# A windowed attention with a channel mix behind it: one small load is added on ScalarE's queue, and the emission of the plan moves out of the block that fixed its order

## The chip, the cores and the metric

The kernel runs on one core of a Trainium2 chip. The metric is device time in microseconds (us) of one execution. Before the change three runs took 165.81, 166.41 and 166.73 us; their median is 166.41 us.

The core has five engines, each with its own stream of instructions: TensorE (PE in the profile, its weight loads PEld), VectorE (DVE), ScalarE (ACT), GpSimd (POOL) and SyncE (SP), which here does nothing but issue DMA transfers. A transfer is issued by the instruction stream of an engine (SPq, ACTq) and carried out by 16 DMA engines that all queues share.

## The reference, cut to what matters

There are 4 batches, 8 heads, 768 positions and a head size of 64. A position sees the first 4 positions (the sinks) and the 128 up to itself (the window). The output of the attention, heads side by side as 512 features, goes into a channel mix with a step back in time.

```python
keep = is_sink | in_window                      # rel >= 0 and rel < 128, or position < 4
a = softmax(where(keep, q @ k.T / 8, -1e9))
x = (a @ v)                                     # heads side by side: [4, 768, 512]
xk = mu_k * x + (1 - mu_k) * x_prev             # x_prev: x one position earlier
xr = mu_r * x + (1 - mu_r) * x_prev
out = sigmoid(xr @ w_r) * (maximum(xk @ w_k, 0) ** 2 @ w_v)
```

## The kernel before, in words

**Tiles.** The work is cut into 12 units u, a batch and a block of 256 positions each. For a unit, `load` (lines 289 to 341) fetches 256 positions of q, k and v for all heads. `prepare` casts them to bf16 and turns q and k so that the head size lies on the partitions: by TensorE with an evacuation (lines 576 and 589), or, for k from u = 4 and q from u = 8 on, by a DMA transpose that SyncE issues (line 562). `attend` makes the scores (line 721), their exponential on ScalarE (line 775), the mask on VectorE (line 789; units 0 and 1 have it as a bias added by TensorE, line 728), the product with v (line 808) and the division (lines 822 and 825). `mix` turns the result (line 849, or by DMA transpose at line 869 for u = 9 to 11) and blends it with its neighbour in time (lines 877 and 888). `ffn` makes the three products: keys (line 939, with relu at 949 or 953 and the square at 963 or 967), gate (line 979, tanh at 985) and values (line 997; line 909 for the very last half), the last step on VectorE (line 1006, 919) and the store (lines 1013 and 924).

**Weights** come as float32 (line 354) and are cast (lines 501 to 507). Their three staging tiles `w32` serve later as result tiles too: line 244 adds their 12 slices to the pool `ob`. That is why the profile calls most result tiles w.

**The plan.** Nothing is issued while these functions run. Each calls `P.op`, which appends an operation to a list: its engine, a closure that emits its instructions, and what it takes and holds. `Plan.run` (line 173) then does two things. It gives every buffer its slot from the written-out list `SLOTS`, so each tile and each PSUM bank has a fixed sequence of users. And it walks the list `ORDER`, a written-out order of all operations on all engines, and emits each one; a negative entry emits a filling matmul on a tile of zeros (`warm`, line 1018). In ORDER the stores of line 1013 stand far behind the operations that make their tiles: all stores but one stand behind the last loads.

**What turns emission into the order on the chip.** Tile, the framework below, finds from the tiles that each instruction reads and writes what has to wait for what, and sets the semaphores. The order of the instructions on one engine can come from two places. In a block `with tc.manual_schedule():` each engine issues its instructions in the order in which they were emitted. Outside such a block Tile's own scheduler chooses: it plays the program through in its own model of the machine, and when an engine is free there, it gets the instruction emitted earliest among those that are ready. On the chip every engine then works through its stream in order, and waits at an instruction whose inputs are not there. Before the change, `P.run()` stands in that block (line 1039), and with it all but the tiles' allocation.

**The start.** On ScalarE's queue the first instructions are two loads of mu (line 374), 4 rows of 128 numbers each, into rows 0 to 7 and columns 384 to 511 of `early`, which is result tile 2 (line 369). The bias of units 0 and 1 lies in other columns of the same tile (lines 371 and 372). Behind the two loads comes the exponential on two numbers (line 384), which loads the activation table. SyncE starts with the loads of k and q of unit 0 (line 337).

Of the kernel before, what the change touches and what calls it, by code (L numbers as in the profile page):

```python
# [185 lines left out]
def kernel(  # L186
# [14 lines left out]
    nc = tc.nc  # L201
    B, H, S, D = q.shape
# [13 lines left out]
    P = Plan()  # L216
# [152 lines left out]
    early = P.pools["ob"][2]  # L369
# [3 lines left out]
    for i, src in enumerate((moe_mu_k, moe_mu_r)):  # L373
        P.op("ACT", 500.0, lambda i=i, src=src: nc.scalar.dma_start(
            out=rows8[NC * i:NC * i + NC, :], in_=src.rearrange("(c p) -> c p", p=128)), -100,
# [660 lines left out]
    ffn(U - 1, 10 * U + FFN_AFTER)  # L1036
    with tc.manual_schedule():
        nc.vector.memset(warm, 0.0)  # L1038
        P.run()


# [33 lines left out]
```

## Time and profile before

| | |
|---|---|
| median of 3 runs | 166.41 us (165.81 to 166.73) |
| the profiled execution | 166.11 us |
| its span, first to last instruction | 164.3 us |
| TensorE clock granted, mean | 0.999 |
| DMA | 79,042 packets, 34.60 MB |

The profile is that of one execution. A group of instructions is named by its line, engine and operation, with the tile it writes, an arrow, and the tiles it reads; x48 is how many there are. A row by stage gives the stretch, its length, and for each engine its busy time and in brackets how many instructions began there, then the granted TensorE clock, the mean busy share of the 16 DMA engines and the GB/s that they moved. A row of waits reads: who waited, for whom, us in total, how often, the longest. A row of the timeline reads: start, duration, engine, line and operation. In the rows of one line or one tile the three numbers between slashes are the shortest, median and longest duration in ns, and after them the first and last start in us.

### The profile page before, as it was taken

What the parts mean: (1) busy time and instruction counts of PE and PEld (TensorE: products, weight loads), DVE (VectorE), ACT (ScalarE), POOL (GpSimd) and SP (SyncE); (2) the same over time, 40 slices, a digit from 0 to 9 for tenths busy, and PEclk for the clock granted to TensorE, in tenths of its full rate; (3) what the DMA queues carried; (4) which work ended last, traced back from release to release, by engine and by line L of the source; (5) the groups of instructions that cost most, each with busy time, mean ns of one, the idle gap of its engine ahead of it and who ended that gap; (6) DMA issues with size and microseconds to landing.
All of it is one profiled execution on the core that took longest, in us unless ns stands there. A gap on an engine that the chain in (4) does not pass through costs nothing.

```text
span 164.3 us, 4195 instructions
## 1 busy us (share of the span) xinstructions
PE 158.4 (96%) x1603; PEld 102.6 (62%) x1603; DVE 145.4 (89%) x381; ACT 131.2 (80%) x218; POOL 13.5 (8%) x38
## 2 busy tenths in 40 slices
PE   6999889999999999999999999999999999999992
PEld 2455568866467587577566775856575765664851
DVE  5259999999999999989999999999999999789752
ACT  3277999999999999999999999997668759163240
POOL 6409300010000000060000000000000000000000
PEclk9999999999999999999999999999999999999999
DMA  4999999999969896999999887986996955077743
GB/s 120 247 305 311 348 335 355 301 354 210 228 154 270 135 240 148 234 198 167 224 216 157 188 156 163 235 146 150 199 123 136 362 149 200 0 90 297 262 185 128
DMA packets 79042, 34.60 MB, mean 211 GB/s; under 512 B 67112, under 2 KB 73520, under 8 KB 79024
## 3 DMA queue, kind: packets, MB, share of 16 engines
q1 hardware_dynamic: 79008, 34.35, 86.3%
q8 instruction: 12, 0.20, 0.6%
q14 instruction: 6, 0.05, 0.1%
q10 hardware_dynamic: 16, 0.00, 0.0%
HBM read 24.12 MB, written 6.29 MB: 185 GB/s over the span
## 4 chain that ended last, share of the span: by engine, by line
PE 79%; ACT 8%; SPq 4%; DMA 3%; issue 2%; DVE 1%; POOL 1%; DVEq 0%; ACTq 0%; POOLq 0%
PE bank L997 23%; PE bank L939 23%; PE bank L979 12%; PE bank L808 6%; PE sc L721 6%; SPq L337 3%; DMA qs<-in_q_dram 3%; PE bank L576 2%; ACT e L775 2%; PE bank L849 2%; ACT rl L949 1%; PE bank L763 1%; ACT qt L589 1%; PE bank L909 1%; PE bank L1018 1%
## 5 line engine op out<-in xcount | busy, mean ns | idle before, releaser
L775 ACT ACTIVATE e<-sc 128x1024 bf16<-128x1024 f32 (+1 forms) x48 | 46.1, 994 | 1.8 <-PE sc L721 1.7
L939 PE MATMUL bank<-xk,wk_sb 128*128 128x256 bf16 x384 | 47.1, 273 | 0.0
L997 PE MATMUL bank<-wv_h,kk 128*128 128x512 bf16 x184 | 43.1, 379 | 0.1
L939 PEld LDWEIGHTS <-wk_sb 128*128 128x128 bf16 x384 | 36.4, 98 | 7.4 <-issue 0.4
L949 ACT ACTIVATE rl<-bank 128x512 bf16<-128x512 f32 x40 | 24.2, 625 | 8.6 <-PE bank L939 7.1
L997 PEld LDWEIGHTS <-kk 128*128 128x128 bf16 x184 | 17.1, 98 | 17.8 <-issue 0.4
L789 DVE TENSOR_TENSOR e<-e,mask 128x1024 bf16<-128x1024 bf16 (+1 forms) x40 | 25.4, 642 | 0.7 <-ACT e L775 0.5
L979 PE MATMUL bank<-wr_sb,xr 128*128 128x512 bf16 x96 | 23.7, 379 | 0.0
L888 DVE SCALAR_TENSOR_TENSOR xk<-td,mu_all,xt 128x256 bf16<-128x256 bf16 x48 | 22.4, 483 | 0.3
L888 DVE SCALAR_TENSOR_TENSOR xr<-td,mu_all,xt 128x256 bf16<-128x256 bf16 x48 | 22.1, 475 | 0.2
L967 ACT ACTIVATE kk<-rl 128x512 bf16<-128x512 bf16 x29 | 18.3, 664 | 4.2 <-DVE rl L953 4.0
L985 ACT ACTIVATE th<-bank 128x512 f32<-128x512 f32 x24 | 15.1, 646 | 5.7 <-PE bank L979 5.7
L825 DVE TENSOR_TENSOR x<-bank,rec 128x256 bf16<-128x256 f32 x48 | 19.2, 416 | 0.4
L808 PE MATMUL bank<-vb,e 128*128 128x65 bf16 x352 | 16.6, 194 | 0.0
L1006 DVE SCALAR_TENSOR_TENSOR w<-th,bank 128x512 f32<-128x512 f32 x19 | 13.0, 682 | 3.6 <-issue 1.8
L808 PEld LDWEIGHTS <-e 128*128 128x128 bf16 x352 | 13.6, 97 | 3.5
L979 PEld LDWEIGHTS <-xr 128*128 128x128 bf16 x96 | 8.8, 98 | 8.6 <-issue 0.2
L721 PE MATMUL sc<-qt,kt 64*128 64x128 bf16 (+1 forms) x256 | 13.9, 238 | 0.0
L721 PEld LDWEIGHTS <-kt 64*128 64x128 bf16 x256 | 8.9, 94 | 5.7 <-issue 3.1
L1018 PE MATMUL bank<-warm 128*128 128x512 bf16 x30 | 10.6, 484 | 1.1 <-DVE warm L1038 1.1
L877 DVE TENSOR_TENSOR td<-xt 128x512 bf16<-128x512 bf16 x24 | 10.3, 428 | 0.7 <-ACT xt L858 0.5
L589 ACT COPY qt<-bank 128x512 bf16<-128x512 bf16 x15 | 9.4, 643 | 1.0 <-PE bank L576 1.0
(74 smaller groups left out, 161.7 us busy)
## 6 DMA issues: line engine op xcount, KB each, us to landing
ks<-in_k_dram SPq DMA_DIRECT2D x24, 256.0 KB, 4.7
qs<-in_q_dram SPq DMA_DIRECT2D x24, 256.0 KB, 4.4
vs<-in_v_dram SPq DMA_DIRECT2D x24, 256.0 KB, 4.4
out_dram<-w SPq DMA_DIRECT2D x19, 256.0 KB, 2.7
w<-in_moe_w_k_dram SPq DMA_DIRECT2D x2, 1024.0 KB, 10.4
w<-in_moe_w_v_dram SPq DMA_DIRECT2D x2, 1024.0 KB, 9.3
w<-in_moe_w_r_dram SPq DMA_DIRECT2D x1, 1024.0 KB, 9.7
out_dram<-ob SPq DMA_DIRECT2D x4, 256.0 KB, 2.6
```

The costliest lines, as they stand in the source:

```text
L721: nc.tensor.matmul(out=sc[:, a, o0:o1], lhsT=lhs[rows], rhs=rhs[rows], start=u not in BIAS, stop=True, skip_group_check=u in BIAS)
L775: nc.scalar.activation(out=buf[ek][:, :, lo:], in_=buf[sck][:, :, lo:], func=AF.Exp, scale=scale)
L789: nc.vector.tensor_tensor(out=at, in0=at, in1=m, op=ALU.mult)
L808: nc.tensor.matmul(out=o[:, g, a, :], lhsT=e[:, a, e0:e0 + 128], rhs=rhs, start=(T == 0 and i == 0), stop=(i == len(blocks) - 1), skip_gro ...
L825: P.op("DVE", dve(256), lambda ok=ok, rk=rk, c=c: nc.vector.tensor_tensor(out=buf["x", u][:, :, 128 * c:128 * c + 128].rearrange("p g (a d ...
L888: nc.vector.scalar_tensor_tensor(out=buf[key][:, c, :], in0=buf[tk][:, i, :], scalar=mu[w][:, c:c + 1], in1=xt[:, c, t0 - 1:t0 + 255], op0 ...
L939: nc.tensor.matmul(out=ps[:, i, :], lhsT=wk_sb[:, c, 128 * f:128 * f + 128], rhs=xk[:, c, :], start=(c == 0), stop=(c == NC - 1), skip_gro ...
L949: nc.scalar.activation(out=buf[rk], in_=buf[psk].rearrange("p (i t) -> p i t", i=2), func=AF.Relu)
L967: nc.scalar.activation(out=buf["kk", u][:, 2 * f2:2 * f2 + 2, :], in_=buf[rk], func=AF.Square)
L979: nc.tensor.matmul(out=buf[psk], lhsT=buf["xr", u][:, c, 128 * g:128 * g + 128], rhs=wr_sb[:, c, :], start=(c == 0), stop=(c == NC - 1))
L985: P.op("ACT", act(512), lambda psk=psk, tk=tk: nc.scalar.activation(out=buf[tk], in_=buf[psk], func=AF.Tanh, scale=0.5), rank + 4 + g, tak ...
L997: nc.tensor.matmul(out=buf[psk], rhs=wv_h[:, f, :], lhsT=buf["kk", u][:, f, 128 * g:128 * g + 128], start=(f == 0), stop=(f == NF - 1))
```

## The change

A transfer is added, and `P.run()` moves one step to the left, out of the block. The transfer reads, for 8 heads and every 16th of the first 256 positions of batch 0, the first 16 numbers of q: 16 rows of 8 runs of 64 bytes, 8 KB. It writes them to rows 16 to 31 and columns 384 to 511 of the tile `early`, where nothing else of the start lies and which nothing reads; much later the tile takes a result. It is the first instruction that the program gives to ScalarE's queue. The block `tc.manual_schedule()` now holds the memset of `warm` and this transfer; everything that `P.run()` emits comes behind the block.

```diff
     ffn(U - 1, 10 * U + FFN_AFTER)
     with tc.manual_schedule():
         nc.vector.memset(warm, 0.0)
-        P.run()
+        nc.scalar.dma_start(
+        out=early[16:32, 384:512].rearrange("p (h d) -> p h d", h=H),
+        in_=q[0, :, 0:256:16, 0:16].rearrange("h p d -> p h d"))
+    P.run()
```

## The prediction

> **What bounds the kernel now.** I began with the share of each engine, then cut the span into stages.
>
> ```profile
> span 164.3 us, 4195 instructions
> ...
> PE 158.4 (96%) x1603; PEld 102.6 (62%) x1603; DVE 145.4 (89%) x381; ACT 131.2 (80%) x218; POOL 13.5 (8%) x38
> ```
> ```profile
> core 0: us, PE busy (x) PEld busy (x) DVE busy (x) ACT busy (x) POOL busy (x), PEclk, DMA share, GB/s
> 0.00:13.00 13.00, 11.75 (x79) 5.48 (x80) 6.08 (x25) 6.09 (x10) 4.99 (x20) 1.00 0.82 225
> 13.00:24.00 11.00, 9.73 (x141) 6.21 (x140) 10.67 (x31) 10.21 (x17) 4.87 (x13) 1.00 1.09 338
> 24.00:47.80 23.80, 23.76 (x236) 15.98 (x236) 23.32 (x59) 23.80 (x39) 0.74 (x2) 1.00 0.98 275
> 47.80:121.50 73.70, 73.59 (x814) 50.01 (x812) 71.32 (x192) 70.44 (x122) 2.89 (x4) 1.00 0.97 185
> 121.50:161.60 40.10, 39.61 (x343) 24.95 (x340) 33.99 (x79) 20.64 (x33) 0.00 (x0) 1.00 0.61 186
> ```
>
> The first line of the page gives the span, 164.3 us; the profiled execution took 166.11 us, so 1.8 us lie around the span, and the median of the three runs, 166.41, is 0.3 above it. My sum is made on 166.1.
>
> The rows by stage say more than the shares. From 47.8 to 121.5 us PE is busy 73.59 of 73.70 us, DVE 71.32, ACT 70.44, and the DMA engines 0.97 of the time. Four resources are full at once. So the order in which each engine takes its work matters: there is no idle engine to take up a bad choice. PE ends the span. Its idle time is 13.00 - 11.75 = 1.25 us before 13 us and 1.27 us from 13 to 24; after that next to nothing until the last products. In the last stage DMA falls to 0.61, and the reason is in the queue that SyncE issues.
>
> ```profile
> L1006 DVE SCALAR_TENSOR_TENSOR w<-th,bank x19: 674/680/689, 47.8 to 159.5; 128x512 f32<-128x512 f32 x19
> L1006 DVE SCALAR_TENSOR_TENSOR ob<-th,bank x4: 677/678/680, 45.6 to 145.6; 128x512 f32<-128x512 f32 x4
> ```
> ```profile
> 0.00:121.50 121.50, 9.37 (x14) 1.00 0.97 221
> 121.50:164.30 42.80, 6.14 (x9) 1.00 0.59 181
> ```
> ```profile
> L1013 SPq DMA_DIRECT2D out_dram<-w x19: 332/564/1017, 121.5 to 160.2; - x19
> L1013 SPq DMA_DIRECT2D out_dram<-ob x4: 398/430/460, 127.5 to 153.2; - x4
> ```
>
> Line 1006 makes the result tiles. The first is made at 45.6 us, and 14 of 23 are made before 121.5 us (the two rows by stage are of line 1006 alone). Yet the first store of line 1013 is issued at 121.5. SyncE's queue holds the stores back until nearly all loads are out, because ORDER puts them there and SyncE takes its instructions in that order.
>
> **The change, part by part.** It has two parts, and the words of its title tell only of one.
>
> *The transfer.* It moves 16 x 8 x 64 bytes: 128 packets on ScalarE's queue, ahead of the two loads of line 374.
>
> ```profile
> 0.81 0.55 ACTq L374 DMA_DIRECT2D ob<-in_moe_mu_r_dram  x1
> 1.40 0.26 ACTq L374 DMA_DIRECT2D ob<-in_moe_mu_k_dram  x1
> 1.69 1.28 ACT L384 ACT_TABLE_LOAD   x1 [1.69 <-PEq L1056]
> 2.98 0.20 ACT L384 ACTIVATE tiny<-warm 128x2 bf16<-128x2 bf16 x1
> 4.84 0.62 ACT L543 CAST kb<-ks 128x512 bf16<-128x512 f32 x1 [1.66 <-DMA ks<-in_k_dram]
> ```
> ```profile
> DMA packets 79042, 34.60 MB, mean 211 GB/s; under 512 B 67112, under 2 KB 73520, under 8 KB 79024
> ...
> q1 hardware_dynamic: 79008, 34.35, 86.3%
> ```
>
> ScalarE spends 0.55 us on the first of its issues; one more puts the table load 0.55 us later, and it then ends at 3.53 instead of 2.98. ScalarE's first real work starts at 4.84, held by the load of k, so 1.66 us of idle time hide this; without them it would cost the 0.55. The two mu loads are late by as much; TensorE's transpose of them is followed by filling matmuls, which hide it. On the DMA engines, q1 spent 86.3% of 16 engines x 164.3 us on 79,008 packets, 28.7 ns each. 128 packets are 3.7 us of one engine, or 0.23 us on all 16. The first k load stands beside them, and the start waits for loads. From nothing (they fit into the idle first microsecond) to 0.9 us (the transfer lands on four engines); I take **0.2 us**, the mean of these packets spread evenly.
>
> The Trainium skill, "DMA: Bandwidth & Descriptors", Specifications, says that transfers under 512 B miss the line rate since the engine reads and modifies before it writes. By that one might double the price, an estimate of 0.5 us; the trace speaks for the smaller one, as 67,112 of its 79,042 packets are under 512 B already and are in the mean.
>
> *The run leaves the ordered region.* `P.run()`, which emits everything else, stood in `tc.manual_schedule()`; now only the memset and the new transfer do. In the region each engine issues in the order of ORDER. Outside it Tile's scheduler sets the order: in its own model of the machine it gives a free engine the earliest emitted instruction that is ready there, so a later one passes an earlier one that still waits. Nothing is computed more or less; instructions change places within an engine. Buffers and banks stay given by SLOTS, and their reuse keeps most of the order, so I expect the bulk to stay. Two things should move.
>
> First the stores. They stand late in ORDER, but are ready long before, and SyncE's queue has holes while it waits for casts before a DMA transpose (line 562):
>
> ```profile
> SPq L562 <- ACT e L775: 4.2, 2, 3.2
> SPq L562 <- ACT rl L949: 4.0, 2, 2.2
> SPq L562 <- ACT kk L967: 2.8, 2, 1.6
> ```
> ```profile
> 155.00:160.00 5.00, 5.00 (x33) 2.95 (x31) 2.68 (x6) 2.31 (x4) 0.00 (x0) 1.00 0.61 231
> ```
>
> The three rows are the longest of SyncE's waits between 47 and 122 us; a store takes such a hole. Its DMA price comes from 155 to 160 us, where only stores flow: 231 GB/s x 5 us = 1.155 MB, or 4.4 stores of 262 KB, in 0.61 x 5 = 3.05 us of all engines: 0.69 us each. 14 stores are 9.7 us that move into 47.8 to 121.5. The free share there is 0.03 x 73.7 = 2.2 us, so loads and transposes behind them come up to 7.5 us late. What covers that is the lead of the loads over their use:
>
> ```profile
> L307 SPq DMA_DIRECT2D vs<-in_v_dram x4: 572/573/580, 109.9 to 125.4; - x4
> L646 DVE CAST vb<-vs x4: 399/419/424, 116.2 to 134.3; 128x512 bf16<-128x512 f32 x4
> ...
> DMA to landing us min/median/max: 3.2/3.7/4.1
> ```
>
> The last v load is issued at 125.4, lands 3.7 later at 129.1, and is cast at 134.3: a lead of 5.2 us. So 7.5 - 5.2 = **2.3 us** reach the path if the load comes late by all of it. Bounds: below nothing (an emptier tail is worth little, as the last store hangs on the last product), above 7.5.
>
> Then the engines' own order. Where an engine waited, the scheduler fills the wait with a later instruction, and what was waited for finds the engine taken. The waits between 24 and 155 us, largest first:
>
> ```profile
> ACT rl L949 <- PE bank L939: 7.1, 6, 3.6
> ACT th L985 <- PE bank L979: 5.2, 3, 3.4
> ...
> ACT kk L967 <- DVE rl L953: 1.6, 2, 1.0
> ...
> DVE rl L953 <- PE bank L939: 1.0, 1, 1.0
> DVE w L1006 <- PE bank L997: 0.9, 2, 0.6
> ACT rl L949 <- ACT kk L967: 0.9, 1, 0.9
> ACT e L775 <- PE sc L721: 0.8, 1, 0.8
> DVE w L1006 <- ACT th L985: 0.7, 1, 0.7
> ```
>
> 13 waits on ACT and 4 on DVE, 18.2 us together. The mean instruction is 131.2 / 218 = 0.60 us on ACT and 145.4 / 381 = 0.38 on DVE; the late comer loses half of one on average: 13 x 0.30 + 4 x 0.19 = 4.7 us. As the scheduler's model is not the chip, new waits come where the model thinks an input is ready and it isn't; the traces show none of these, so the bound above is the 18.2 us once more. Below it is a gain: the 1.25 + 1.27 = 2.5 us that PE idles before 24 us. I take **3.4 us**, about three quarters of 4.7, as waits that lie in slack (behind a full PE) cost nothing.
>
> The sum: 0.2 + 2.3 + 3.4 = 5.9; 166.1 + 5.9 = **172.0 us**.
>
> The start has one more risk.
>
> ```profile
> L1018 PE MATMUL bank<-warm x30: 379/384/634, 1.1 to 23.8; 128*128 128x512 bf16 x30
> ```
>
> The 30 filling matmuls of line 1018 stand between real ones; ready early, they may bunch up ahead and leave PE idle before the real work. The earliest of them take 634 ns against a median of 384, though the granted clock reads 1.00. The Trainium skill, "TensorE: Matmul & The Clock Gate", Part 1, says that an idle window of some 3.4 us halves TensorE's clock for about as long again; by that the sum would be an estimated 1.7 us more (half of 3.4). The 634 ns at the start agree with a slow start; no later row shows one.
>
> **The rivals.**
>
> *The order hardly changes* (not slower). Emission order is the scheduler's own priority, and one bank or buffer has one order of users in any case. If its model is close to the chip, each engine gets nearly ORDER back, and only the transfer is left: 166.1 + 0.2 = 166.3. For it speaks PE's full row, 73.59 of 73.70: where nothing waits, nothing is passed. Against it, the 14 stores that are ready up to 76 us before their issue.
>
> *Passing helps* (faster). PE's 2.5 us of early idle time are filled by work that stood behind a blocked one, and early stores cost nothing, since shares near 1.0 count packets under way rather than bytes: the start runs at 338 GB/s, the middle at 185. It decides if the DMA engines carry the 14 stores without delay to a transpose. 166.1 - 2.5 = 163.6.
>
> *The transposes are late* (much slower). From u = 4 on k goes through a DMA transpose that SyncE issues in turn. If a store stands ahead of each, all 9.7 us reach PE, with the full 4.7 of the order: 166.1 + 0.2 + 9.7 + 4.7 = 180.7. For it speaks DMA at 0.97; against it, the 5.2 us of lead.
>
> **How the numbers follow.** A difference under 0.5% (0.8 us) is about what a measurement of this kernel can't tell from no change. Forecast, 168 to 177 us: 0.61. Order hardly changes: 0.11, all within 0.5%. Passing helps: 0.12, faster. Late transposes, beyond 177: 0.16. So faster 0.12, same 0.11, slower 0.77. The range is 165.5 to 181. Its upper end is the late transposes' 180.7, which lies above the sum with the upper bound of the stores and all of the order (166.1 + 0.9 + 7.5 + 4.7 = 179.2). Its lower end takes in the case in which the order hardly changes, and the upper part of the faster one; what is left out, most of the faster case and waits beyond the 4.7, I hold at some 0.17.
>
> **What would show it.** In the profile after: stores of line 1013 issued from about 48 us on, and DMA share from 121.5 on well under 0.61, show the first step; if the first is still near 121 us, it is wrong. PE busy in 47.8 to 121.5 falling by 2 to 6 us, with new waits on ACT and DVE, shows the second. Line 543's first cast of k still at about 4.8 us shows the transfer hidden. The prediction is wrong if the instruction order of ACT, DVE and SyncE is unchanged, or if PE stays full while the order differs.

## The result

The changed kernel takes 195.09 us (median of four runs, 193.52 to 196.60), the kernel before 166.21 beside it (165.81 to 166.73). The ratio is 1.170, with a 95% interval of 1.165 to 1.174: 28.9 us slower, where 5.9 were forecast. The sign was right, the size far off. One of the four runs, 196.60 us, was slow, at a granted clock of 0.965; the ratios leave such runs out and the medians do not, and without them the medians would be 194.01 here, 192.76 in e2, 180.88 in e3, 175.29 in e4, 183.44 in e14, and within 0.2 us of those given in the other runs. The first lines of the page after:

```profile
span 191.9 us, 4187 instructions
...
PE 166.8 (87%) x1603; PEld 104.5 (54%) x1603; DVE 146.2 (76%) x381; ACT 132.9 (69%) x218; POOL 11.7 (6%) x38
```

The same instructions ran, and those of DVE and ACT took as long as before: 146.2 us against 145.4, 132.9 against 131.2. The span is 27.6 us longer. On DVE and ACT nearly all of that is idle time. On PE 19.2 us of it are (5.9 us idle before, 25.1 after); the other 8.4 are busy time, 158.4 to 166.8 us for the same 1603 matmuls, and what made these longer was not tried. The rows by stage of the changed kernel. The first two stages are those of before. The third ends at SyncE's first DMA transpose (before at 42.6, after at 54.0), the fourth near the last load of v (125.4 and 137.3):

```profile
0.00:13.00 13.00, 11.14 (x78) 5.13 (x78) 6.02 (x24) 5.84 (x10) 7.02 (x29) 1.00 0.79 214
13.00:24.00 11.00, 8.01 (x99) 4.66 (x96) 9.46 (x23) 8.16 (x12) 1.98 (x3) 1.00 1.06 342
24.00:54.00 30.00, 24.61 (x253) 16.06 (x253) 23.21 (x61) 25.27 (x40) 0.39 (x2) 1.00 0.72 204
54.00:136.70 82.70, 77.24 (x801) 50.05 (x800) 69.89 (x186) 69.69 (x122) 2.32 (x4) 0.98 0.91 173
136.70:191.90 55.20, 45.84 (x383) 28.63 (x381) 37.64 (x90) 23.98 (x37) 0.00 (x0) 1.00 0.51 139
```

PE, which was full from 24 us on, now idles in every stage: 3.0 us from 13 to 24, 5.4 from 24 to 54, 5.5 in the long middle, 9.4 at the end. From 54 us on DVE and ACT idle more still (DVE 12.8 and 17.6 us, ACT 13.0 and 31.2). On the stretch for which the prediction named a number, and the one behind it:

```profile
47.80:121.50 73.70, 68.04 (x672) 43.56 (x667) 62.21 (x162) 61.62 (x107) 2.32 (x4) 0.98 0.78 154
121.50:161.60 40.10, 36.20 (x387) 23.12 (x385) 33.28 (x87) 28.41 (x45) 0.00 (x0) 1.00 0.95 212
```

PE lost 5.6 us from 47.8 to 121.5, as forecast (2 to 6). But that is 5.6 of the 19.2 us by which its idle time grew, so the agreement says little. And DMA share there fell from 0.97 to 0.78, where early stores should have filled it, and rose behind it. The stores tell why:

```profile
L1013 SPq DMA_DIRECT2D out_dram<-w x19: 332/447/643, 134.8 to 187.9; - x19
```

The first store is issued at 134.8, not at 48: it moved 13.3 us *later*. The waits of ACT and DVE, longest first (rows of other engines left out):

```profile
ACT rl L949 <- PE bank L939: 14.8, 10, 5.9
ACT th L985 <- PE bank L979: 9.5, 8, 5.8
DVE rec L822 <- PE bank L808: 7.7, 7, 2.1
...
ACT rl L949 <- DVE ob L1006: 6.2, 1, 6.2
ACT kk L967 <- DVE rl L953: 5.8, 4, 2.5
...
ACT e L775 <- PE sc L721: 4.1, 5, 1.7
DVE rec L822 <- ACT qt L589: 4.0, 1, 4.0
```

Four of these pairs stood in the list before too, with 7.1, 5.7, 4.0 and 1.7 us (lines 949, 985, 967 and 775). The other three are new or were half a microsecond at most: DVE and ACT now stand at an instruction whose input is not there.

### The profile page after: what moved, and what is told of

It is laid out like the page before. It is cut to its first block, busy times and chain, and to the rows that moved or that the text cites. A ratio compares the mean times of both kernels' runs of the same rounds, so it can differ in the third digit from the quotient of the medians.

```text
span 191.9 us, 4187 instructions
## 1 busy us (share of the span) xinstructions
PE 166.8 (87%) x1603; PEld 104.5 (54%) x1603; DVE 146.2 (76%) x381; ACT 132.9 (69%) x218; POOL 11.7 (6%) x38
## 5 line engine op out<-in xcount | busy, mean ns | idle before, releaser
L939 PE MATMUL bank<-xk,wk_sb 128*128 128x256 bf16 x384 | 48.5, 275 | 3.7 <-DVE rl L953 2.4
L775 ACT ACTIVATE e<-sc 128x1024 bf16<-128x1024 f32 (+1 forms) x48 | 43.9, 965 | 4.1 <-PE sc L721 4.1
L997 PE MATMUL bank<-wv_h,kk 128*128 128x512 bf16 x184 | 44.0, 379 | 2.5 <-DVE w L1006 1.9
L888 DVE SCALAR_TENSOR_TENSOR xk<-td,mu_all,xt 128x256 bf16<-128x256 bf16 x48 | 21.6, 477 | 0.0
L985 ACT ACTIVATE th<-bank 128x512 f32<-128x512 f32 x24 | 14.4, 612 | 9.9 <-PE bank L979 9.5
L808 PE MATMUL bank<-vb,e 128*128 128x65 bf16 x352 | 18.0, 196 | 2.5 <-ACT qt L589 0.7
L808 PEld LDWEIGHTS <-e 128*128 128x128 bf16 x352 | 14.5, 99 | 9.2 <-issue 3.6
L822 DVE RECIPROCAL rec<-bank 128x4 f32<-128x4 f32 x48 | 8.0, 176 | 13.8 <-PE bank L808 7.7
L721 PE MATMUL sc<-qt,kt 64*128 64x128 bf16 (+1 forms) x256 | 15.8, 240 | 1.3 <-ACT e L775 0.7
L721 PEld LDWEIGHTS <-kt 64*128 64x128 bf16 x256 | 9.9, 95 | 8.5 <-issue 6.6
```

Of the source, the lines that this page charges most:

```text
L721: nc.tensor.matmul(out=sc[:, a, o0:o1], lhsT=lhs[rows], rhs=rhs[rows], start=u not in BIAS, stop=True, skip_group_check=u in BIAS)
L775: nc.scalar.activation(out=buf[ek][:, :, lo:], in_=buf[sck][:, :, lo:], func=AF.Exp, scale=scale)
L808: nc.tensor.matmul(out=o[:, g, a, :], lhsT=e[:, a, e0:e0 + 128], rhs=rhs, start=(T == 0 and i == 0), stop=(i == len(blocks) - 1), skip_gro ...
L888: nc.vector.scalar_tensor_tensor(out=buf[key][:, c, :], in0=buf[tk][:, i, :], scalar=mu[w][:, c:c + 1], in1=xt[:, c, t0 - 1:t0 + 255], op0 ...
L939: nc.tensor.matmul(out=ps[:, i, :], lhsT=wk_sb[:, c, 128 * f:128 * f + 128], rhs=xk[:, c, :], start=(c == 0), stop=(c == NC - 1), skip_gro ...
L985: P.op("ACT", act(512), lambda psk=psk, tk=tk: nc.scalar.activation(out=buf[tk], in_=buf[psk], func=AF.Tanh, scale=0.5), rank + 4 + g, tak ...
```

## The experiments

All but e2 and e16 hold the added transfer. The streams of instructions that are compared below are those of the compiled programs, engine by engine.

**e1 and e2: each part alone.** e1 keeps the transfer and leaves `P.run()` in the block; e2 moves `P.run()` out and has no transfer.

```diff
 e1:  with tc.manual_schedule():
          nc.vector.memset(warm, 0.0)
+         nc.scalar.dma_start(...)
          P.run()
 e2:  with tc.manual_schedule():
          nc.vector.memset(warm, 0.0)
-         P.run()
+     P.run()
```

> The transfer as in the change, with P.run() back inside the ordered block. Theory 'order': the whole loss comes from the order in which the engines take their work, so this is within 0.8 us of the kernel before, about 166.4. Rival 'transfer': the transfer delays the loads of the start and with them everything behind, so a good part of the 28 us stays, say 175 or more.

> P.run() outside the ordered block, without the transfer. Theory 'order': 193 to 197 us, as in the changed kernel. Rival 'transfer': clearly under that. A third reading, that both are needed (the transfer late on a queue whose order is bad): between 166 and 193.

e1: 167.13 us (ten runs), ratio 1.0052 (1.0022 to 1.0082). e2: 194.58, ratio 1.162 (1.152 to 1.171). So the transfer costs 0.9 us and leaves the other instructions in their order; the rest, some 27 to 28 us, comes with leaving the block. Below, each kernel is compared with e1's 167.13.

The 0.9 us have a place. PE's start, before:

```profile
3.99 0.24 PE L486 MATMUL bank<-ident,ob 8*128 8x8 f32 x1
4.17 3.03 PE L1018 MATMUL bank<-warm 128*128 128x512 bf16 x7
7.04 0.39 PE L576 MATMUL bank<-ident,kb 128*128 128x128 bf16 x4
```

and in e1:

```profile
4.70 0.24 PE L486 MATMUL bank<-ident,ob 8*128 8x8 f32 x1 [0.82 <-DMA ob<-in_moe_mu_k_dram]
4.87 3.17 PE L1018 MATMUL bank<-warm 128*128 128x512 bf16 x7
...
8.26 1.49 PE L728 MATMUL sc<-ob,ident 128*128 128x384 bf16 x4
...
10.39 0.49 PE L576 MATMUL bank<-ident,qb 128*128 128x128 bf16 x4
```

The mu loads stand behind the transfer and land later, PE's transpose of mu (line 486) stalls 0.82 us, and the slow matmuls last longer: the four of line 728 take 1.49 us, against 0.81 before. The first transposes of qb come at 10.39, against 8.35.

**e3, e4, e5: a stretch of ORDER.** One stretch of ORDER's 1,082 entries is emitted outside the block, all the rest inside it (`part(a, b)` walks `ORDER[a:b]`). The diff is e5's; e3 has only the entries before 340 outside, e4 only those from 932 on:

```diff
     with tc.manual_schedule():
         ...
-        P.run()
+        P.part(0, 340)
+    P.part(340, 932)
+    with tc.manual_schedule():
+        P.part(932, None)
```

> Only the first 340 entries of ORDER (up to the first DMA transpose of k) are left to the scheduler; the rest is in the ordered block. In the changed kernel the first DMA transpose starts at 53.98 us instead of 42.58, and from there to the last load of v the distance is as before. Theory 'start and drain': the start is worth 11 to 12 us and stays lost to the end, 176 to 180. Rival 'spread': each stretch costs by its length, so 340 of 1082 entries cost a third of 28 us, about 9, of which some is caught up, 170 to 175. Rival 'drain': a delay of the start is caught up in the middle, under 170.

> Only the entries of ORDER from 932 on (from the last load of v on) are left to the scheduler. In the changed kernel the last load of v is 11.9 us late and the end 27.6. Theory 'start and drain': 12 to 16 us are lost here, 178 to 182. Rival 'carried over': the drain is long because what went before left the units in another state, and its own order costs little, 166 to 170. Rival 'spread': 150 of 1082 entries cost about 4 us, 170.

> The transfer stays; of ORDER's entries only 340 to 931 (from about 40 to 125 us) are emitted outside the ordered block, start and end inside it. Theory A (the order costs where engines run dry, in the start and in the drain; in the middle the full queues carry it): start alone was 182.26 and end alone 176.03 against 167.13 with all in order, 15.1 and 8.9 together 24.0 of the 28.0 that the change loses beyond the transfer; 4.0 are left, so 167 to 171 us. Rival B (my step as predicted: 17 waits of the middle, each losing half an instruction, and stores moving early): 167.1 + 3.4 + 2.3 = 172.8. Rival C (every stretch costs about the same per operation): 592 of 1,260 entries, 13 to 15 us more, 180 to 182. The stores' step is right if a store of line 1013 appears before 110 us.

(ORDER has 1,082 entries, not 1,260; rival C's share comes to 15 us all the same.) Measured: start 182.26 (+15.1), end 176.03 (+8.9), middle 176.91 (+9.8). The three add to 33.8 us, more than the 28.0 of all at once. None of the three came out inside a range that was written down for it. Theory A fell: the full queues of the middle do not carry it. The prediction's 172.8 did not hold either, nor did rival C's 180 to 182. How a free start loses is seen in e3's stages:

```profile
24.00:48.00 24.00, 20.66 (x211) 13.37 (x212) 16.94 (x45) 19.70 (x31) 0.39 (x2) 0.93 0.87 250
48.00:54.00 6.00, 4.89 (x45) 2.73 (x42) 6.00 (x16) 5.09 (x8) 0.00 (x0) 1.00 0.00 0
```

From 48 to 54 us no byte moves. The changed kernel has the same hole: SyncE's queue in time, and its longest wait there:

```profile
41.97 0.60 SPq L307 DMA_DIRECT2D vs<-in_v_dram  x1
53.98 1.29 SPq L562 DMA_TRANSPOSE kt<-kb  x1
```
```profile
SPq L562 <- DVE kb L536: 17.3, 3, 11.4
```

SyncE stands for 11.4 us at the first DMA transpose, for a cast that VectorE reaches at 53.5 us, and the loads behind it wait as well. The free middle (e5) hides its loss better: its last load of v is issued at 124.2, *earlier* than in e1 (127.2), but work was left behind, and PE waits for it later:

```profile
120.00:130.00 10.00, 9.64 (x92) 6.42 (x92) 8.05 (x23) 5.33 (x9) 0.00 (x0) 1.00 1.05 159
130.00:140.00 10.00, 7.48 (x74) 4.82 (x73) 9.34 (x22) 4.57 (x7) 0.00 (x0) 1.00 0.34 118
```

**e6 to e10 and e12: one engine.** The block can fix the order of some engines only. In e6 to e10 all but one are fixed, in e12 only VectorE is.

```diff
-    with tc.manual_schedule():
+    with tc.manual_schedule(engines={PE, Activation, Pool, SP}):   # e6
```

> All is emitted in the ordered block with the transfer, but VectorE alone is left out of the fixed order; the four other streams keep theirs. Theory A1 (VectorE's late cast of kb, L536, holds SyncE's first DMA transposes and with them all loads behind): the first L562 moves from 44.4 to some 54 us as it did in the changed kernel, DMA share near 0 in 48 to 53 us, and the time rises by about 10 of the 28 us or more: 177 to 187. Rival A2 (it is TensorE's order, with groups of products torn apart, and VectorE only follows): the first L562 within 2 us of 44.4 and the time 167 to 171.

> All is emitted in the ordered block with the transfer, but TensorE alone is left out of the fixed order; the four other streams keep theirs. Theory A1 (VectorE's order decides): 167 to 172 us, as a TensorE whose products are swapped still finds its inputs in the old order. Rival A2 (TensorE's own order decides): 178 us or more, with idle time of TensorE in the start and behind 137 us as in the changed kernel. Passing as a gain (one of the prediction's rivals): under 166.

> All is emitted in the ordered block with the transfer, but SyncE's queue of loads, DMA transposes and stores alone is left out of the fixed order. The step on the stores as predicted: stores of line 1013 from about 48 us on, and 167.1 + 2.3 = 169.4 us (up to 174.6 with the bound of 7.5). Rival: the scheduler lets the stores stand near 121 us here too, and the time is 167 us within 0.5.

> With the transfer; ScalarE alone is left out of the fixed order. Alone, VectorE's order cost 13.3 us over the 167.1 of the transfer alone, TensorE's 5.0 and SyncE's some 2. Theory (the cost comes from the loaded engines that feed TensorE, about in proportion to their share): ScalarE is as loaded as VectorE from 24 to 110 us, so 5 to 10 us, 172 to 177. Rival (only VectorE's order matters, as it makes what TensorE and SyncE wait for): under 169.

> With the transfer; GpSimd alone is left out of the fixed order. Theory: GpSimd is busy only 13.5 us, but it casts q and k of unit 1 between 13 and 20 us, and in the changed kernel its masks go ahead of them; that delays TensorE once, by the 1.5 us or so of those masks: 168 to 170. Rival (GpSimd's work has slack): 167.1 within 0.5.

> The changed kernel, with VectorE alone kept in ORDER's order and the four other engines left to the scheduler. If the losses of the engines add up, 195.1 - 13.3 = 182 us. If they compound (an engine whose own order waits for another's late work loses more than alone), less than that: 174 to 178. If VectorE's order cost so much only because the others were fixed, and a free set adapts to one another, more: 188 or above.

| left to the scheduler | us | over e1 | ratio to before (95%) |
|---|---|---|---|
| e6, VectorE | 180.38 | 13.3 | 1.085 (1.082 to 1.088) |
| e9, ScalarE | 178.31 | 11.2 | 1.075 (1.071 to 1.078) |
| e7, TensorE | 172.12 | 5.0 | 1.036 (1.033 to 1.040) |
| e8, SyncE | 169.21 | 2.1 | 1.015 (1.011 to 1.020) |
| e10, GpSimd | 167.22 | 0.1 | 1.006 (1.003 to 1.008) |
| e12, all but VectorE | 182.00 | 14.9 | 1.097 (1.093 to 1.100) |

The five add to 31.7 us; all at once cost 28.0. And e12 came out at the 182 that a plain sum gives (195.1 - 13.3). For VectorE this holds whichever way it is taken: its order costs 13.3 us with the others fixed and 13.1 with the others free (195.09 - 182.00). The other four do not add up as well: 18.4 us alone, 14.9 together. Of the ranges, e7 came out at the edge of A1's, e9 above its theory's (the rival, under 169, is out), and e10 as its rival said: GpSimd's work has slack.

e6 shows that A1 had the size right and the cause wrong: the first DMA transpose moves only from 44.4 to 47.9 us, yet 13.3 are lost. What PE waited for in e6, longest first:

```profile
PE bank L576 <- DVE kb L543: 2.5, 2, 1.4
PE bank L939 <- DVE x L825: 1.9, 3, 0.8
PE bank L997 <- DVE w L1006: 1.6, 1, 1.6
PE bank L939 <- DVE rl L953: 1.5, 1, 1.5
```

No row stands out: casts, divisions, results, relus. All rows of PE that name DVE, but for the memset of warm at the start, come to 11.7 us, near the 13.3; e1 has one such row, of 0.4 us.

In e8 the stores behave nearly as in ORDER: the first at 117.2 us (e1: 123.3), none at 48. The rival is right on their place. The time rose all the same, by 2.1 us; in the profiled execution PE has one new wait, 3.4 us of line 721 for a DMA transpose of k, and the granted clock is 0.50 from 119 to 125 us. That execution took 173.58 us, so what brought the 2.1 us of the median stays open.

**e11 and e16: the start.** PE's transpose of mu moves 17 entries down ORDER, behind the first four matmuls of line 728, with the transfer (e11) and without it (e16).

```diff
-    ..., 77, -1, -2, -3, -4, -1, -2, 90, 0, 1, 79, 102, ...
-    -2, -3, -4, -2, 103, 104, 2, 3, 119, 105, ...
+    ..., 77, -1, -2, -3, -4, -1, -2, 0, 1, 79, 102, ...
+    -2, -3, -4, -2, 103, 104, 2, 3, 119, 90, 105, ...
```

> With the transfer and everything in the ordered block; TensorE's transpose of mu (line 486) stands 13 entries later in TensorE's stream, behind the first four of line 728. Theory (the transfer costs its 0.9 us because the mu loads land 0.7 us later, TensorE's transpose of mu then stalls 0.82 us, and a TensorE that has idled keeps its slow matmuls until some 10.4 us instead of 7.0): no stall, first fast group at about 7.0 us, time as before, 166.0 to 166.4, ratio 1.000 within 0.002. Rival (the packets on the DMA engines cost it, the step as predicted): 166.9 to 167.1, ratio 1.005.

> The kernel before, without the transfer, with TensorE's transpose of mu 13 entries later. In the run with the transfer that made TensorE's first filling matmuls fast, but then TensorE waited 1.03 us for the cast of q at 8.35 us, as late as before. Theory (the load of q sets the start): same as before, 165.9 to 166.4. Rival (a shorter start reaches the end): 165.0 to 165.6.

e11: 166.05 us in twelve runs, ratio 0.9995 (0.9975 to 1.0014). The transfer is still there, with all its packets, and its cost is gone; so the packets were not the cost, the stalled transpose of mu was. e16: 166.15, ratio 1.001 (0.999 to 1.003): no gain without the transfer. e11's trace shows why:

```profile
1.13 4.29 PE L1018 MATMUL bank<-warm 128*128 128x512 bf16 x13 [1.13 <-DVE warm L1038]
...
8.35 0.40 PE L576 MATMUL bank<-ident,qb 128*128 128x128 bf16 x4 [1.03 <-DVE qb L543]
```

PE is done with its first work early and then waits for the cast of q, which ends when it did before. No version here beats the kernel before.

**e13, e14: which instructions of VectorE?** When VectorE alone is free, 188 of its 381 instructions stand later than in ORDER, by 568 places together. Reciprocals are on the mean 2.9 and divisions 2.5 places late, blends and casts of v go ahead. From here on ORDER is rewritten so that only VectorE's stream differs from e1's. A piece of it (e13):

```diff
 L543 TensorCopy qb_84<-qs_72
+L888 TensorScalarPtr xr_117<-td_110,mu_all,xt_155
 L822 Reciprocal rec_104<-bank_65
 L680 TensorTensor vsink_153<-bank_64,hmask
 L825 TensorTensor x_107<-bank_65,rec_104
 L543 TensorCopy qb_84<-qs_72
-L888 TensorScalarPtr xr_117<-td_110,mu_all,xt_155
```

and of e14, where the same kinds stay and the others go:

```diff
+L822 Reciprocal rec_104<-bank_65
+L680 TensorTensor vsink_153<-bank_64,hmask
 L543 TensorCopy qb_84<-qs_72
-L822 Reciprocal rec_104<-bank_65
-L680 TensorTensor vsink_153<-bank_64,hmask
 L825 TensorTensor x_107<-bank_65,rec_104
```

> With the transfer and all in the ordered block; ORDER is rewritten so that the streams of TensorE, ScalarE, SyncE and GpSimd are the same to the last instruction, and on VectorE only the blends (L888) and the casts of v (L646) stand at the place that the scheduler gave them in the run with VectorE free, on the mean 1.8 and 3.8 places earlier; each kind they pass falls back by about one place (reciprocals L822 1.0, divisions L825 1.4). Theory (VectorE's order costs because work with slack goes ahead of the divisions that TensorE waits for): half of the 13.3 us of VectorE or more, 173 to 181. Rival (the loss is spread over all kinds of instructions alike): these are 109 of 367, so about 4 us, 169 to 172.

> As the run before, but the other way round: on VectorE the reciprocals, divisions, blends and casts of v stand at their places of ORDER, and all else stands where the scheduler put it (as near as the order of inputs allows). Theory: what cost VectorE its 13.3 us is gone, 167 to 170 us. Rival (spread over all kinds): 162 of 367 instructions still stand elsewhere, so about 6 us stay, 172 to 175.

e13: 170.26 us (+3.1). e14: 183.85 (+16.7), slower than with all of VectorE's order left to the scheduler. Both speak against the theory. e13 lies in its rival's range, 169 to 172: blends and casts of v that go ahead carry little by themselves. e14 lies above both of its ranges. There the loss is even larger than in e6, though fewer places are out of order (214 of lateness against 568). Either the other kinds (casts, masks, results, relus) carry the loss, or half of one order and half of another fit neither; these two runs do not tell which.

**e15, e17, e18: lateness by itself.** In e15 each of the 96 reciprocals and divisions comes up to three places later, as far as the inputs allow (262 places together); in e18 one place (96); in e17 each of the 96 blends up to three (275). Pieces of e15 and e17:

```diff
 e15:  L822 Reciprocal rec_101<-bank_64
       L825 TensorTensor x_107<-bank_64,rec_101
 -     L822 Reciprocal rec_102<-bank_66
       L825 TensorTensor x_107<-bank_66,rec_102
 -     L543 TensorCopy qb_83<-qs_71
 e17: +L822 Reciprocal rec_103<-bank_66
      +L589 TensorCopy qt_90<-bank_63
      +L825 TensorTensor x_107<-bank_66,rec_103
       L888 TensorScalarPtr xr_117<-td_110,mu_all,xt_155
       L888 TensorScalarPtr xk_113<-td_110,mu_all,xt_155
```

> With the transfer and all in the ordered block; on VectorE each of the 48 reciprocals (L822) and 48 divisions (L825) stands three places later and what they let pass comes earlier; the other streams are the same. The scheduler had them 2.9 and 2.5 places later. Three places are 3 x 0.38 = 1.1 us. Theory (lateness of the divisions is what costs): 10 us or more, 177 to 185. Rival (TensorE has other work in its stream while it waits, so a division may be late by 1 us): under 170.

> The control to the late divisions: with the transfer and all in the ordered block, the 96 blends (L888) each stand three places later on VectorE, and what they let pass comes earlier; the other four streams are the same. 96 instructions are moved as far as in the run with the late divisions (28.3 us slower). Theory (what costs is a late reader of a bank: the four banks of PSUM pass from product to product, and a product that needs the bank waits; a blend reads no bank): 167 to 171 us. Rival (any order other than ORDER costs by how far it is displaced): 180 or more.

> The late divisions in a smaller dose: each of the 96 one place later instead of three. Theory (no slack: the loss goes with the lateness): a third of 28.3, 9.4 us, 176 to 177. Rival (a bank has slack, so that a short delay is hidden and only what goes beyond it costs): 167 to 171.

e15: 195.46 us (+28.3): as slow as the changed kernel, from one engine's two lines, and far above the theory's 177 to 185. e18: 175.48 (+8.4), close to the third that the theory gave: for these lines there is no slack that hides a short delay. PE's waits in e15, then in e18:

```profile
PE bank L939 <- DVE x L825: 6.9, 5, 2.1
PE bank L979 <- DVE x L825: 4.0, 3, 1.9
PE bank L849 <- DVE x L825: 3.7, 6, 1.1
```
```profile
PE bank L849 <- DVE x L825: 2.6, 7, 0.8
PE bank L939 <- DVE x L825: 1.6, 2, 1.3
PE bank L979 <- DVE x L825: 1.1, 1, 1.1
```

The products of lines 939 and 979 do not read x. They wait because the division is the last reader of the bank that they are to write: four banks go from product to product. That made me think that only readers of a bank are dear. e17 was the control, and it refuted that: 192.43 us (+25.3) for blends, which read no bank. Its waits of PE:

```profile
PE bank L939 <- DVE xk L888: 10.2, 13, 1.8
PE bank L979 <- DVE xr L888: 5.9, 5, 1.5
```

Here the products wait for their input. Late by a bank or late by an operand, PE pays alike. Per place of lateness that comes to 8.4 us / 96 = 0.087 us in e18, 28.3 / 262 = 0.108 in e15 and 25.3 / 275 = 0.092 in e17, about a quarter of the 0.38 us that a place on VectorE lasts. The scheduler's own order is gentler, 13.3 / 568 = 0.023 on VectorE and 11.2 / 262 = 0.043 on ScalarE. And the number of places is no price by itself. In e13 instructions of VectorE come some 265 places late too (counted in the traces of e1 and e13, the instructions of a kind taken in order), nearly as many as in e15, and 3.1 us are lost, 0.012 a place; in e14 it is 16.7 / 214 = 0.078. Which instructions come late matters as much as how far.

## Why the prediction was wrong, step by step

**What bounds the kernel:** right. PE full, with DVE and ACT nearly so from 24 us on, and no idle engine to take up a bad choice. I then did not draw the consequence.

**The engines' order, 3.4 us: the step that failed.** Everything but the transfer cost some 27 to 28 us (28.0 from 167.13 to 195.09), and the single engines' orders give 31.7 in all. The step counted 17 waits of the kernel before and charged each half an instruction. (Its list stopped at 0.7 us; the shorter waits of ACT and DVE would have added ten and 2.4 us, which changes little.) But the scheduler does not only fill old waits: when VectorE alone is free, it puts 188 of 381 instructions later, and late ones make new waits: in e6 PE waits 11.7 us for DVE where it waited 0.4 in e1, and in e18 a single place of lateness already has its price. My text said that new waits would come and put their bound at 18.2 us; the range's upper end was then made with 4.7, not with that bound. With it the sum would have been 166.1 + 0.2 + 2.3 + 18.2 = 186.8, or 192.7 with the upper bounds of the transfer and the stores (0.9 and 7.5), and still missed 195.1: old waits say nothing of how many new ones there will be. The free middle (some 40 to 125 us), most of the stretch from which I took the waits, cost 9.8 us alone (e5), the free start 15.1 (e3).

**The stores, 2.3 us:** the mechanism did not occur. In the changed kernel the first store is at 134.8 us, and the earliest of any run at 107.8 (e4), none near 48. SyncE's order costs 2.1 us alone (e8), near my number by luck and not for its reason, which would have needed stores from 48 us on.

**The transfer, 0.2 us:** it cost 0.9 (e1), the upper end of its bounds. Its reason was wrong. It is not the packets; it is the 0.7 us by which the mu loads come late, which PE's transpose of mu meets unprotected (e11). I wrote that the filling matmuls behind the transpose hide that; they stand behind it in PE's stream, so they wait too. In the changed kernel itself the scheduler starts line 486 at 6.12 us, without a stall, and e2, which has no transfer, takes 194.58 us against 195.09: whether the 0.9 is part of the 28.9 at all is not shown. ScalarE's part was right. Its start in the changed kernel:

```profile
0.81 0.41 ACTq L1039 DMA_DIRECT2D ob<-in_q_dram  x1
...
2.38 1.28 ACT L384 ACT_TABLE_LOAD   x1 [2.38 <-issue]
3.68 0.20 ACT L384 ACTIVATE tiny<-warm 128x2 bf16<-128x2 bf16 x1
5.21 0.62 ACT L543 CAST kb<-ks 128x512 bf16<-128x512 f32 x1 [1.32 <-DMA ks<-in_k_dram]
```

The table load is 0.69 us later, its wait absorbs that, and the first cast still hangs on the load of k (in e1 at 4.90, before at 4.84).

**The start's risk:** the filling matmuls did bunch up, but not to harm: e7, where TensorE's order is free, has its first scores at 9.4 us, before at 9.5, e1 at 11.7. The clock is taken up below.

**The rivals.** The order changed on every engine, so the first is out. Passing as a gain is out on each of the five engines: none was faster alone. The late transposes are in the trace (SyncE's 11.4 us), but through a late cast, not through stores ahead of them.

**What stays open.** Which of VectorE's 188 late instructions cost the 13.3 us: e13 and e14 show only that blends and casts of v going ahead are not the bulk of it. Why the scheduler ranks as it does: its model of the machine was not tried. And whether leaving the block costs anything besides the order: no run emits the scheduler's whole order inside the block. Against it speaks that e14, e15 and e17 lose 16.7 to 28.3 us inside the block, by VectorE's order alone.

## What to carry to other kernels

When three engines are full at once, the order of each is part of the work: the waits that are there now do not price a change of order, since late instructions make new ones. The number of places by which instructions come late gives no more than an order of size: here a place on VectorE cost 0.01 to 0.11 us, as it hit one instruction or another. Freeing one engine at a time gave a better price, as the engines' losses nearly added up (31.7 us against 28.0). Before a load is put ahead of others on a queue, look for the first instruction on the bottleneck engine that waits for those others; and if it is not urgent, move it back, as e11 did.

## What the runs showed of the hardware

PE's clock falls without PE being idle for a whole stretch. Two rows by stage of the changed kernel:

```profile
58.60:62.00 3.40, 1.56 (x18) 0.94 (x16) 0.00 (x0) 3.37 (x7) 0.00 (x0) 1.00 1.12 223
62.00:65.30 3.30, 3.30 (x34) 2.57 (x35) 1.75 (x8) 1.50 (x3) 0.00 (x0) 0.51 0.92 210
```

PE is busy 1.56 of 3.40 us, and the granted clock is 0.51 for the next 3.3 us, under a full PE. The prediction found no such row in the trace of before. The Trainium skill, "TensorE: Matmul & The Clock Gate", Part 1, speaks of an idle window of some 3.4 us that halves the clock. The half agrees, and so does the length of the slow stretch; but the stretch of 3.40 us ahead of it was 46% busy. Nor does that share decide by itself: in the same trace PE is busy 1.57 us from 174.67 to 178.09, and the clock stays at 1.00. In the profiled execution the mean granted clock is 0.991, so 0.009 x 191.9 = 1.7 us of clock are lost; in the other three it was 0.982, 0.965 and 0.974, which makes at most 0.035 x 194.6 = 6.8 us. The clock is a part of the loss, and not the 28 us: e15's profiled execution loses as much at a granted clock of 1.00.

At the start the granted clock reads 1.00 while matmuls run slow, and how long that lasts differs between executions of nearly the same start. In e11 six filling matmuls begin between 3.6 and 4.8 us; in e16, with no gap on PE either, four do. The ten from 2.4 us on take 4.47 us in e16, and 3.04 in e11:

```profile
2.38 4.47 PE L1018 MATMUL bank<-warm 128*128 128x512 bf16 x10
6.65 0.61 PE L576 MATMUL bank<-ident,kb 128*128 128x128 bf16 x4
```

The Trainium skill, "TensorE: Matmul & The Clock Gate", Part 1, says that the window runs freely and does not begin with the kernel, so that the point of change moves from run to run; these two starts agree. But the stall at line 486 moves it too. The record of the clock in each trace begins with the first full clock, and before that entry the views print 1.00. In the eight traces without a stall it begins between 3.8 and 7.1 us (before 6.9, e11 3.8, e16 7.1). In the twelve where PE stands 0.8 to 1.2 us ahead of line 486 it begins between 8.6 and 10.6 us (e1 10.6), but for e18, where it begins at 4.0, ahead of the stall. So the 10.4 us of e1's profile lie at the late end of what the stall brings, and e1's median of ten runs is the number to hold on to.
